# One group ahead instead of two: reordering the software pipeline of a two-layer attention and feed-forward kernel

## Chip, cores, metric

One core of one Trainium2 chip. The metric is the time of one execution on the device, in microseconds (us), as a median of several runs. One execution per kernel was also recorded by the hardware profiler; its span is about 2 us below the time of the same execution. PE is TensorE, DVE VectorE, ACT ScalarE, POOL GpSimd, SP the engine that issues most DMAs.

## The reference, cut

Two layers, each an attention block A and a feed-forward block B with residuals, with the same weights in both layers; sequence 2048, width 1024, 32 heads of 32, hidden width 3584, bf16. Attention looks at eight positions only: itself and 2, 4, ... 14 back.

```python
idx = pos[:, None] - off[None, :]            # off = 0, 2, ..., 14
logits = einsum("bhsd,bhswd->bhsw", q, kg) * scale   # kg, vg: gathered windows of k, v
attn = softmax(where(mask, logits, -1e9))
o = einsum("bhsw,bhswd->bhsd", attn, vg)
x = x + A(layernorm(x)); x = x + B(layernorm(x))     # B: gelu(x @ w1 + b1) @ w2 + b2
x = x + A(layernorm(x)); x = x + B(layernorm(x))
```

## The kernel before

The sequence is cut in four groups of T = 512 positions; a step n is one group in one layer, so there are eight steps. Everything is kept transposed (features on partitions). Nearly all matmuls stream 512 columns. The parts of a step:

- *Layernorm*: sums by matmuls with a matrix of ones, `s1` (centring, DVE), `s2` (squares, ACT, and their sums, PE), `s3` (Ln, Exp on ACT, scaling in two halves on DVE).
- *Projections* `gen_qkv`: 8 chunks of q and k, then 8 of v (24 "units" of 8 matmuls). For each q, k chunk DVE builds the products for all eight window positions, and PE reduces them over a head with a 128x32 stationary matrix, four tiles side by side.
- *Value part* `av_chunk`, 8 chunks: the softmax weights go to DRAM and come back by a broadcast DMA (1 MB a chunk), DVE multiplies them with the windows of vT and adds the eight positions up.
- *Output projection* `gen_wo`, then FFN1 (28 units) and FFN2 (16 units).

```python
xnp = tile_pool(bufs=2); attp = tile_pool(bufs=1)     # kT and vT: one buffer each
wpool = tile_pool(bufs=4); prodp = tile_pool(bufs=2); abcp = tile_pool(bufs=3)
def acc_tile(): return psum.tile([P, T], F32, name="acc", bufs=4)
for g in range(NG):                                   # all x loads first, on the SP queue
    nc.sync.dma_start_transpose(xg[g][:], ...)
...
def av_a(n, c):                                       # cut
    d = ABC_Q.dma_start(abc[...], src)                # broadcast, paced by PE progress (mark)
    nc.vector.tensor_tensor(out=abc[:], in0=abc[:], in1=win(vT[:, c, :]), op=ALU.mult)
def av_b_dve(n, c):                                   # three adds: 8 -> 4 -> 2 -> 1 positions
...
def pipelined():                                      # run(gen, sides): sides[u] is issued after unit u
    ln_a[0].all()
    run(gen_qkv(0, ...), layernorm of step 1)
    run(gen_qkv(1, ...), layernorm of step 2, av_chunk(0, c) at unit 2c)
    for n in range(N):
        if n + 2 < N:
            if n >= 1:
                run(gen_ffn1(n - 1, ...), av_chunk(n + 1, c) at units 1, 6, 11, ...)
                run(gen_ffn2(n - 1), last av_chunks, first layernorm of step n + 2)
            run(gen_wo(n))
            run(gen_qkv(n + 2, ...), second layernorm of step n;   # for n == 0 also
                                     av_chunk(1, c) at unit 2c)
        ...                                           # the two last steps: cut
```

So the value part of step n+1 is done one round before its output projection. Instructions are then placed on their engines by a scheduler that may move ready work forward; each engine runs its list in order.

Of the kernel before, what the change touches and what calls it, by code (L numbers as in the profile page):

```python
# [18 lines left out]
def kernel(  # L19
# [56 lines left out]
    prodp = ctx.enter_context(tc.tile_pool(name="prodp", bufs=2))  # L76
    smp = ctx.enter_context(tc.tile_pool(name="smp", bufs=1))
    abcp = ctx.enter_context(tc.tile_pool(name="abcp", bufs=3))
    hpool = ctx.enter_context(tc.tile_pool(name="hpool", bufs=1))
    iop = ctx.enter_context(tc.tile_pool(name="iop", bufs=1))  # L80
    psum = ctx.enter_context(tc.tile_pool(name="psum", bufs=1, space=PSUM))
    dram = ctx.enter_context(tc.tile_pool(name="dram", bufs=2, space=DRAM))

# [17 lines left out]
    last_pe = [None]  # L101
    mark = [None]
# [5 lines left out]
    PE_AV = False  # L108
    last_seg = [None]
# [19 lines left out]
    for g in range(NG):  # L129
        nc.sync.dma_start_transpose(xg[g][:], x_in[g * T:(g + 1) * T, :].rearrange("s (k p) -> s k p", p=P))  # L130
# [4 lines left out]
    nc.vector.memset(eps_t[:], EPS)  # L135
    smat = const.tile([P, NCH, H], BF16, name="smat")
# [17 lines left out]
    with nc.allow_non_contiguous_dma(reason="tiny bias loads"):  # L154
        nc.sync.dma_start(b1_bf[:], B_b1.rearrange("(j p) -> p j", p=P))
        nc.sync.dma_start(b2_bf[:], B_b2.rearrange("(j p) -> p j", p=P))
    b1T = const.tile([P, KF], F32, name="b1T")
    b2T = const.tile([P, KD], F32, name="b2T")
    nc.vector.tensor_copy(b1T[:], b1_bf[:])
    nc.vector.tensor_copy(b2T[:], b2_bf[:])  # L160
# [13 lines left out]
    def rstd_from(src, prev, preload):  # L174
        rstd = lnp.tile([P, T], F32, name="rstd", bufs=2)
        if preload:
            pl = nc.scalar.preload_act_table_set(LN_SET)
            dep_order(pl, prev, "table preload after squares")
            prev = pl
        ln_i = nc.scalar.activation(rstd[:], src, ACT.Ln, bias=eps_t[:], scale=1.0 / D)  # L180
        dep_order(ln_i, prev, "ln after squares/preload")
        nc.scalar.activation(rstd[:], rstd[:], ACT.Exp, scale=-0.5)  # L182
        return rstd

    class LN:
        def __init__(self, g, preload=False):
            self.g = g
            self.xn = None
            self.preload = preload

        def s1(self):
            x = xg[self.g]
            ps_sum = aux_f32()
            for c in range(KD):
                mm(ps_sum[:], lhsT=ones_bf[:], rhs=x[:, c, :], start=(c == 0), stop=(c == KD - 1))
            self.xn = xnp.tile([P, KD, T], BF16, name="xn")
            nc.vector.scalar_tensor_tensor(  # L197
                out=self.xn[:], in0=ps_sum[:].unsqueeze(1).to_broadcast([P, KD, T]), scalar=-1.0 / D,
                in1=x[:], op0=ALU.mult, op1=ALU.add)

        def s2(self):
            xn = self.xn
            self.ps_sq = aux_f32()
            for c in range(KD):
                sq = lnp.tile([P, T], BF16, name="sq", bufs=2)
                self.last_sq = nc.scalar.activation(sq[:], xn[:, c, :], ACT.Square)  # L206
                mm(self.ps_sq[:], lhsT=ones_bf[:], rhs=sq[:], start=(c == 0), stop=(c == KD - 1))

        def s3(self):
            xn = self.xn  # L210
            rstd = rstd_from(self.ps_sq[:], self.last_sq, self.preload)
            KH2 = KD // 2
            for hh in range(2):
                nc.vector.tensor_tensor(out=xn[:, hh * KH2:(hh + 1) * KH2, :], in0=xn[:, hh * KH2:(hh + 1) * KH2, :],  # L214
                                        in1=rstd[:].unsqueeze(1).to_broadcast([P, KH2, T]), op=ALU.mult)
            self.ps_sq = None
# [26 lines left out]
    def gen_qkv(n, ln, v_first):  # L243
# [56 lines left out]
        pending = None  # L300
        for c4 in range(NCH // 4):
            wq = load_w(wqkv_v, c4 * 4 * P)
            wk = load_w(wqkv_v, D + c4 * 4 * P)
            for cc in range(4):
                c = c4 * 4 + cc
                psq = gemm_chunk(wq, cc, xn, KD)
                qT = qp.tile([P, T], BF16, name="qT")
                nc.scalar.copy(qT[:], psq[:])  # L308
                yield
                psk = gemm_chunk(wk, cc, xn, KD)  # L310
                nc.scalar.copy(kT[:, c, HALO:], psk[:])  # L311
                prod = prodp.tile([P, W, T], BF16, name="prod")
                nc.vector.tensor_tensor(out=prod[:], in0=qT[:].unsqueeze(1).to_broadcast([P, W, T]), in1=win(kT[:, c, :]), op=ALU.mult)  # L313
                if pending is not None:
                    qk_reduce(*pending)
                pending = (c, prod)
                yield
        if g + 1 < NG:
            nc.scalar.copy(khalo[:], kT[:, :, T:T + HALO])
        if v_first:  # L320
            stn["finish"] = (lambda pend=pending: finish(pend))
        else:
            yield from v_part(after_first=(lambda pend=pending: finish(pend)))

    def av_a(n, c):
        stn = st[n]
        vT = stn["vT"]
        a_d = stn["a_d"]
        if c == 0:
            stn["oT"] = attp.tile([P, NCH, T], BF16, name="oT", bufs=2)  # L330
            stn["abc"] = {}
        abc = abcp.tile([P, W, T], BF16, name="abc")
        for hi in range(HPC):
            src = a_d[HPC * c + hi:HPC * c + hi + 1, :, :].rearrange("o w t -> o (w t)").to_broadcast([DH, W * T])
            d = ABC_Q.dma_start(abc[hi * DH:(hi + 1) * DH, :, :].rearrange("p w t -> p (w t)"), src)  # L335
            if mark[0] is not None:
                dep_sync(d, mark[0], "pace abc broadcast with PE progress")
        nc.vector.tensor_tensor(out=abc[:], in0=abc[:], in1=win(vT[:, c, :]), op=ALU.mult)  # L338
        stn["abc"][c] = abc

    def av_b_dve(n, c):
        stn = st[n]
        pv = stn["abc"].pop(c)
        oT = stn["oT"]
        nc.vector.tensor_tensor(out=pv[:, 0:4, :], in0=pv[:, 0:4, :], in1=pv[:, 4:8, :], op=ALU.add)  # L345
        nc.vector.tensor_tensor(out=pv[:, 0:2, :], in0=pv[:, 0:2, :], in1=pv[:, 2:4, :], op=ALU.add)  # L346
        nc.vector.tensor_tensor(out=oT[:, c, :], in0=pv[:, 0, :], in1=pv[:, 1, :], op=ALU.add)

    def av_b_pe(n, c):
        stn = st[n]  # L350
        pv = stn["abc"].pop(c)
        oT = stn["oT"]
        ps = acc_tile()
        for w_ in range(W):
            mm(ps[:], lhsT=ident[:], rhs=pv[:, w_, :], start=(w_ == 0), stop=(w_ == W - 1))
        nc.scalar.copy(oT[:, c, :], ps[:])
# [18 lines left out]
    def gen_ffn1(n, ln):  # L375
        xn = ln.xn
        hT = hpool.tile([P, KF, T], BF16, name="hT")
        st[("h", n)] = hT
        for j4 in range(KF // 4):
            wt = load_w(w1_v, j4 * 4 * P)  # L380
            for jj in range(4):
                j = j4 * 4 + jj
                ps = gemm_chunk(wt, jj, xn, KD)
                nc.scalar.activation(hT[:, j, :], ps[:], ACT.Gelu_apprx_tanh, bias=b1T[:, j:j + 1])  # L384
                yield

    def gen_ffn2(n):
# [3 lines left out]
        for i2 in range(KD // 2):  # L391
            pss = [acc_tile(), acc_tile()]
            for kh in range(2):
# [3 lines left out]
                for ii in range(2):  # L397
                    for k in range(KH):
                        m = mm(pss[ii][:], lhsT=w2t[:, k, ii * P:(ii + 1) * P], rhs=hT[:, kh * KH + k, :],
                               start=(kh == 0 and k == 0), stop=(kh == 1 and k == KH - 1))  # L400
                        if k == 0:
                            mark[0] = m
                    if kh == 1:
                        i = i2 * 2 + ii
                        nc.vector.scalar_tensor_tensor(out=x[:, i, :], in0=pss[ii][:], scalar=b2T[:, i:i + 1], in1=x[:, i, :],  # L405
                                                       op0=ALU.add, op1=ALU.add)
                    yield
# [22 lines left out]
    def seq_all():  # L430
        for n in range(NSTEP):
# [22 lines left out]
    def ln_sides(sides, ln, u0, du):  # L454
        add_side(sides, u0, ln.s1)
        add_side(sides, u0 + du, ln.s2)
        add_side(sides, u0 + 2 * du, ln.s3)

    def pipelined():
        N = NSTEP  # L460
        ln_a = {}
        ln_b = {}
        nc.scalar.preload_act_table_set(LN_SET)
        ln_a[0] = LN(0)
        ln_a[0].all()
# [7 lines left out]
        for c in range(NCH):  # L473
            if PE_AV:
                add_side(sides, 2 * c, (lambda c=c: av_a(0, c)))
                add_side(sides, 2 * c + 5, (lambda c=c: av_b_pe(0, c)))
# [3 lines left out]
        for n in range(N):  # L480
            g = n % NG
            has_qkv = (n + 2 < N)
            if has_qkv:
                if n >= 1:
# [18 lines left out]
                    ln_sides(sides, ln_a[n + 2], 5, 3)  # L503
# [7 lines left out]
                if n == 0:  # L511
                    ln_sides(sides, ln_b[n], 2, 4)
                    for c in range(NCH):
                        if PE_AV:
                            add_side(sides, 2 * c, (lambda c=c: av_a(1, c)))
                            add_side(sides, 2 * c + 5, (lambda c=c: av_b_pe(1, c)))
# [7 lines left out]
            elif n == N - 2:  # L524
# [12 lines left out]
                ln_sides(sides, ln_b[n], 1, 3)  # L537
# [17 lines left out]

    if NG >= 4 and NSTEP >= 4:
        pipelined()
    else:
        seq_all()
# [30 lines left out]
```

## Time and profile before

| | before |
|---|---|
| median of 4 runs | 1437.43 us (1436.34 to 1438.71) |
| PE busy | 1333.3 us, 93% of the span |
| first projection matmul | 30.3 us |
| PE waits of over 20 us | 34.6 us (to 158.6), 26.9 us (to 254.4) |

From the page of the kernel before: first the busy time by engine, then three rows of the span in 40 slices of 36 us, each digit the busy share in tenths (PEclk is the granted clock of TensorE in tenths).

```profile
PE 1333.3 (93%) x6413; PEld 590.5 (41%) x6542; DVE 715.4 (50%) x540; ACT 412.4 (29%) x648; POOL 147.6 (10%) x337
...
PE   4994593999999999999999999999999999999996
...
DVE  3669589436663467336673376444574274201000
...
PEclk7997797899999999999999999999999999999998
```

PE is full from the ninth slice to the last but one. Nearly all its waste lies in the first eight slices and at the end. The waits of PE name it (columns: engine, tile, line waiting, then what released it; us in total, times, longest):

```profile
PE acc L123 <- ACT vT L288: 61.4, 2, 34.6
...
PE acc L123 <- DMA wt<-in_B_w_dram: 2.7, 1, 2.7
```

The two value-eviction waits are two holes in the prologue (the time before the first feed-forward matmuls). The windows view shows who worked meanwhile (busy us and instructions of PE, PEld, DVE, ACT, POOL, then clock, DMA share and GB/s):

```profile
124.00:158.60 34.60, 0.03 (x2) 0.00 (x0) 34.15 (x29) 1.88 (x4) 10.09 (x20) 0.53 0.66 162
226.30:254.40 28.10, 1.27 (x6) 0.49 (x5) 27.49 (x25) 1.84 (x4) 8.15 (x16) 0.60 0.74 173
265.50:1102.00 836.50, 831.95 (x4007) 368.99 (x4087) 448.59 (x337) 254.60 (x402) 94.15 (x190) 1.00 0.77 196
```

In both holes DVE is over 97% busy and PE is all but empty. Most of DVE's work there is the value part of the step before; in the first hole the rest is the softmax of step 1 and the scaling of step 2's layernorm:

```profile
124.48 2.28 DVE L214 TENSOR_TENSOR xn<-xn,rstd 128x2048 bf16<-128x2048 bf16 x1
...
134.67 2.29 DVE L214 TENSOR_TENSOR xn<-xn,rstd 128x2048 bf16<-128x2048 bf16 x1
```

vT has one buffer, so the v chunks of the next step cannot leave their four accumulators until the last product of the step before has read vT; with four accumulators full PE stops. After 265 us the same engines overlap and PE idles half a per cent.

One more reading, the start of an output projection in the steady state, first PE, then DVE (start, duration):

```profile
527.17 13.98 PE L123 MATMUL acc<-oT,wt 128*128 128x512 bf16 x62
...
535.44 0.42 DVE L347 TENSOR_TENSOR oT<-abc 128x512 bf16<-128x512 bf16 x1
```

The last oT of the newer step is begun 8.3 us and done 8.7 us after this output projection began. Harmless here: it uses the oT of the older step.

### The profile page before, as it was taken

What the parts mean: (1) busy time and instruction counts of PE and PEld (TensorE: products, weight loads), DVE (VectorE), ACT (ScalarE), POOL (GpSimd) and SP (SyncE); (2) the same over time, 40 slices, a digit from 0 to 9 for tenths busy, and PEclk for the clock granted to TensorE, in tenths of its full rate; (3) what the DMA queues carried; (4) which work ended last, traced back from release to release, by engine and by line L of the source; (5) the groups of instructions that cost most, each with busy time, mean ns of one, the idle gap of its engine ahead of it and who ended that gap; (6) DMA issues with size and microseconds to landing.
All of it is one profiled execution on the core that took longest, in us unless ns stands there. A gap on an engine that the chain in (4) does not pass through costs nothing.

```text
span 1437.2 us, 15240 instructions
## 1 busy us (share of the span) xinstructions
PE 1333.3 (93%) x6413; PEld 590.5 (41%) x6542; DVE 715.4 (50%) x540; ACT 412.4 (29%) x648; POOL 147.6 (10%) x337
## 2 busy tenths in 40 slices
PE   4994593999999999999999999999999999999996
PEld 1341241444444444444444444444434444444443
DVE  3669589436663467336673376444574274201000
ACT  2332130421243113431144123432134210720411
POOL 1022122120011100121002100121003010000000
PEclk7997797899999999999999999999999999999998
DMA  9377488699359962899449973699638885455551
GB/s 234 118 200 191 121 205 212 165 234 229 128 158 245 232 198 88 223 244 223 138 147 243 236 202 117 184 246 220 196 116 224 230 196 175 143 144 168 169 144 40
DMA packets 277349, 263.17 MB, mean 183 GB/s; under 512 B 28960, under 2 KB 266528, under 8 KB 269088
## 3 DMA queue, kind: packets, MB, share of 16 engines
q1 hardware_dynamic: 263968, 192.96, 48.0%
q0 software_dynamic: 13312, 69.22, 21.9%
q8 instruction: 51, 0.84, 0.3%
q14 instruction: 18, 0.15, 0.0%
HBM read 251.67 MB, written 6.29 MB: 179 GB/s over the span
## 4 chain that ended last, share of the span: by engine, by line
PE 84%; DVE 8%; DMA 4%; issue 2%; ACT 1%; SPq 1%; DVEq 0%; ACTq 0%
PE acc L123 78%; PE aux L123 3%; DMA wt<-in_B_w_dram 3%; DVE abc L338 3%; PE L L123 2%; DVE prod L313 1%; DVE abc L345 1%; SPq L130 1%; DVE xn L197 1%; DVE abc L346 1%; DVE xn L214 1%; DMA out_dram<-xio 0%; PE aux L126 0%; DMA b_bf<-in_B_b_dram 0%; ACT xio L171 0%
## 5 line engine op out<-in xcount | busy, mean ns | idle before, releaser
L123 PEld LDWEIGHTS <-wt 128*128 128x128 bf16 x5632 | 547.5, 98 | 746.5 <-issue 104.0
L123 PE MATMUL acc<-xn,wt 128*128 128x512 bf16 x3247 | 742.1, 382 | 68.8 <-ACT vT L288 61.4
L123 PE MATMUL acc<-hT,wt 128*128 128x512 bf16 x1760 | 393.7, 379 | 1.8
L384 ACT ACTIVATE hT<-acc,b1T 128x512 bf16<-128x512 f32 x224 | 153.1, 687 | 259.1 <-PE acc L123 251.2
L338 DVE TENSOR_TENSOR abc<-abc,vT 128x4096 bf16<-128x4096 bf16 x64 | 146.3, 2287 | 156.6 <-DMA abc<-a_d 156.6
L313 DVE TENSOR_TENSOR prod<-qT,kT 128x4096 bf16<-128x4096 bf16 x64 | 146.0, 2289 | 83.7 <-ACT kT L311 83.7
L405 DVE SCALAR_TENSOR_TENSOR xg<-acc,b2T,xg 128x512 bf16<-128x512 f32 x64 | 48.0, 749 | 278.1 <-PE acc L123 278.0
L335 POOL DMA_DIRECT2D abc<-a_d x256 | 124.4, 495 | 510.6 <-PE acc L123 320.8
L206 ACT ACTIVATE sq<-xn 128x512 bf16<-128x512 bf16 x128 | 73.0, 623 | 181.7 <-DVE xn L197 135.1
L123 PE MATMUL acc<-oT,wt 128*128 128x512 bf16 x500 | 112.5, 379 | 0.6
L214 DVE TENSOR_TENSOR xn<-xn,rstd 128x2048 bf16<-128x2048 bf16 x32 | 73.0, 2285 | 40.6 <-ACT rstd L182 40.6
L197 DVE SCALAR_TENSOR_TENSOR xn<-aux,xg 128x4096 bf16<-128x4096 f32 x16 | 70.8, 4424 | 43.7 <-PE aux L123 35.9
L371 DVE TENSOR_TENSOR xg<-acc,xg 128x512 bf16<-128x512 f32 x64 | 44.1, 690 | 79.4 <-PE acc L123 76.8
L308 ACT CAST qT<-acc 128x512 bf16<-128x512 f32 x64 | 37.5, 586 | 147.0 <-PE acc L123 139.9
L345 DVE TENSOR_TENSOR abc<-abc 128x2048 bf16<-128x2048 bf16 x64 | 78.3, 1223 | 1.8
L276 POOL DMA_DIRECT2D a_d<-a x32 | 18.6, 618 | 502.9 <-DVE a L273 502.9
L123 PE MATMUL aux<-sq,ones_bf 128*128 128x512 bf16 x128 | 47.3, 392 | 12.7 <-ACT sq L206 12.5
L311 ACT CAST kT<-acc 128x512 bf16<-128x512 f32 x64 | 37.4, 584 | 68.4 <-PE acc L123 63.8
L288 ACT CAST vT<-acc 128x512 bf16<-128x512 f32 x64 | 36.8, 586 | 62.9 <-PE acc L123 62.3
L123 PEld LDWEIGHTS <-ones_bf 128*128 128x128 bf16 x256 | 25.6, 100 | 54.7 <-issue 27.7
L171 ACT COPY xio<-aux 128x1024 bf16<-128x1024 bf16 x16 | 16.2, 1011 | 110.1 <-PE aux L126 84.0
L346 DVE TENSOR_TENSOR abc<-abc 128x1024 bf16<-128x1024 bf16 x64 | 44.1, 689 | 1.7
(43 smaller groups left out, 251.4 us busy)
## 6 DMA issues: line engine op xcount, KB each, us to landing
abc<-a_d POOLq DMA_DIRECT2D x256, 256.0 KB, 8.0
wt<-in_B_w_dram SPq DMA_DIRECT2D x56, 1024.0 KB, 5.9
wt<-in_B_w_dram SPq DMA_DIRECT2D x64, 896.0 KB, 10.4
wt<-in_A_wqkv_dram SPq DMA_DIRECT2D x48, 1024.0 KB, 5.1
wt<-in_A_wo_dram SPq DMA_DIRECT2D x16, 1024.0 KB, 5.8
out_dram<-xio SPq DMA_DIRECT2D x16, 256.0 KB, 2.2
a_d<-a POOLq DMA_DIRECT2D x32, 64.0 KB, 2.4
xg<-in_A_x_dram SPq DMA_TRANSPOSE x4, 6.4
```

Source lines behind the costliest of these rows:

```text
L123: return pe_chain(nc.tensor.matmul(out_ap, *args, **kwargs), _seg(out_ap))
L197: nc.vector.scalar_tensor_tensor(out=self.xn[:], in0=ps_sum[:].unsqueeze(1).to_broadcast([P, KD, T]), scalar=-1.0 / D, in1=x[:], op0=ALU.m ...
L206: self.last_sq = nc.scalar.activation(sq[:], xn[:, c, :], ACT.Square)
L214: nc.vector.tensor_tensor(out=xn[:, hh * KH2:(hh + 1) * KH2, :], in0=xn[:, hh * KH2:(hh + 1) * KH2, :], in1=rstd[:].unsqueeze(1).to_broadc ...
L313: nc.vector.tensor_tensor(out=prod[:], in0=qT[:].unsqueeze(1).to_broadcast([P, W, T]), in1=win(kT[:, c, :]), op=ALU.mult)
L335: d = ABC_Q.dma_start(abc[hi * DH:(hi + 1) * DH, :, :].rearrange("p w t -> p (w t)"), src)
L338: nc.vector.tensor_tensor(out=abc[:], in0=abc[:], in1=win(vT[:, c, :]), op=ALU.mult)
L345: nc.vector.tensor_tensor(out=pv[:, 0:4, :], in0=pv[:, 0:4, :], in1=pv[:, 4:8, :], op=ALU.add)
L346: nc.vector.tensor_tensor(out=pv[:, 0:2, :], in0=pv[:, 0:2, :], in1=pv[:, 2:4, :], op=ALU.add)
L371: nc.vector.tensor_tensor(out=x[:, i, :], in0=ps[:], in1=x[:, i, :], op=ALU.add)
L384: nc.scalar.activation(hT[:, j, :], ps[:], ACT.Gelu_apprx_tanh, bias=b1T[:, j:j + 1])
L405: nc.vector.scalar_tensor_tensor(out=x[:, i, :], in0=pss[ii][:], scalar=b2T[:, i:i + 1], in1=x[:, i, :], op0=ALU.add, op1=ALU.add)
```

## The change

The intent: work one step ahead instead of two. The prologue then needs one projection stage whose vector work finds no feed-forward matmuls to hide behind, not two. With it come a shorter start (one x load first, biases later, the first layernorm in two column halves), reductions in batches of two chunks, and pins that keep layernorm matmuls at their place. Cut to what runs (options that are off, and helpers for them, are left out):

```diff
-    prodp = tile_pool(name="prodp", bufs=2)
+    prodp = tile_pool(name="prodp", bufs=3)
+    ONE_AHEAD = True
+    RED_BATCH = 2
+    OT_BUFS = 1 if ONE_AHEAD else 2
-    for g in range(NG):
-        nc.sync.dma_start_transpose(xg[g][:], ...)
+    load_x(0)
-    nc.sync.dma_start(b1_bf[:], ...); nc.sync.dma_start(b2_bf[:], ...)
+    def load_bias():   # on the POOL queue, called later
 ...
                 nc.scalar.copy(kT[:, c, HALO:], psk[:])
+                if len(pending) >= RED_BATCH:
+                    flush(0)                    # reduce both waiting chunks
                 prod = prodp.tile([P, W, T], BF16, name="prod")
 ...
-                if pending is not None:
-                    qk_reduce(*pending)
-                pending = (c, prod)
+                pending.append((c, prod))
 ...
+    def pipelined1():
+        lnA = LN(0, cols=(0, T // 2)); lnB = LN(0, cols=(T // 2, T), xn=lnA.xn)   # s1, s2, s3 in turn
+        run(gen_qkv(0, ...), load_x(1), (2), (3) at units 2, 4, 6; layernorm of step 1)
+        run(gen_qkv(1, ...), av_chunk(0, c) at unit 2c;
+                             gen_wo(0) and the second layernorm of step 0 at unit 19)
+        for n in range(1, N):
+            run(gen_ffn1(n - 1, ...), av_chunk(n, c) at units 1, 6, 11, ...)
+            run(gen_ffn2(n - 1), last av_chunks, first layernorm of step n + 1)
+            run(gen_wo(n))
+            run(gen_qkv(n + 1, ...), second layernorm of step n)
+            # the last step: av_chunks every 3.7 units of FFN1, gen_wo in the middle of FFN2,
+            # that FFN2's residual adds pinned behind the last oT
```

## The prediction

> **What bounds it now.** TensorE: the page has PE busy 1333 of 1437 us, and in the windows from 265 to 1422 us it idles about 1%, at clock 1.00 nearly throughout. Its waste (windows, PE waits): the start, 30.3 us before the first projection matmul; two holes, 124 to 158.6 and 227 to 254.4 us, put down to the value eviction (34.6 and 26.9 us); 2.7 us for a weight DMA at 1123; a 15 us tail. In both holes the vector engine is over 97% busy: vT has one buffer, so the value projection of group n+1 waits for group n's last vT product (2.29 us each, 4.6 with its adds, eight per group).
>
> **What the change does.**
> 1. One group ahead, not two. Hole 1 stays, but group 1's value products now spread over FFN1/FFN2 of group 0, as later groups' did already. Hole 2 goes: -27 us, and -2 of cold clock after it (0.78 granted there). The Trainium skill, "TensorE: Matmul & The Clock Gate", Part 1: idleness throttles the clock, activity releases it; the trace agrees.
> 2. Hole 1 loses group 2's layernorm from its vector queue (4.42 + 2 x 2.29 us): -7.
> 3. New exposure: group 0's output projection and second layernorm stand before FFN1 with only half a value projection behind them. Estimate from trace durations: residual add 0.7, sums 0.5, centring 4.4, squares and sums 5.9, Ln and Exp 1.4, first scaling 2.3 = 15 us, less 7 us of value matmuls: +9.
> 4. Start. One x load comes first; the vector queue no longer waits for biases (until 23.5 us, then it ran group 1's centring ahead of group 0's scaling); group 0's layernorm runs in column halves. First projection at 22 to 24 us: -7, of which 2 come back as group 1's layernorm matmuls now run among projections: -5.
> 5. Reduction in batches of two. Eight reduction matmuls with their switches take 0.65 us of each 4.10 us pair; two rounds of four at 0.216 are 0.43. The Trainium skill, "TensorEngine Tiling (Array Packing)", Key Properties, says a mode change drains the array; the timeline agrees. Half of 64 switches at 0.2 us: -6.
> 6. The steady state does the same matmuls, but a group's output projection now follows directly on its own value products. In before's timeline the last oT is done at 535.4 us, 8 us after the output projection began (527.2), harmless as that used the older group. Matmuls of k = 0 to 6 in four accumulators (28 x 0.216 = 6 us) can hide most: +5 over six groups.
> 7. End: value products every 3.7 FFN1 units, before every 3: -1.
>
> **Sum.** 1437 - 29 - 7 + 9 - 5 - 6 + 5 - 1 = 1403; with some luck in ordering, 1400 us (-2.6%), range 1380 to 1428. Faster by over 2%: 0.68; within 2%: 0.30; slower: 0.02.
>
> **What would show it.** One value-eviction wait of 25 to 30 us in place of two; a new PE idle of 5 to 12 us before the first FFN1, released by the layernorm; first projection at 22 to 24 us; reductions in runs of 16; PE busy sum nearly unchanged; at each output projection a PE wait for oT under 3 us.
>
> **What would make it wrong.** Step 6: if the vector queue puts the last products behind FFN2's residual adds and the matmul order has no filler, each group stalls 5 to 8 us: +30, and the gain is gone. Step 4: if the later x transposes (4.2 us of issue each) hold up weight loads in their queue, 5 to 7 us come back. Step 2: if value products are paced by their broadcast DMA, hole 1 does not shrink.

## The result, and the profile after

The changed kernel takes 1404.44 us (median of 9 runs, 1401.88 to 1411.86), the kernel before 1438.10 us (median of 12). The ratio is 0.9771, with a 95% interval of 0.9754 to 0.9788. Ratios here and below are the mean time of one kernel's fast runs over that of the other's of the same rounds, so not quite the ratio of the medians.

The page after, the same rows:

```profile
PE 1330.6 (95%) x6430; PEld 594.3 (42%) x6558; DVE 719.5 (51%) x544; ACT 408.7 (29%) x654; POOL 149.5 (11%) x339
...
PE   6991799999999999999999999999999999899996
...
DVE  4769543764446733567336663466444674633000
...
PEclk8996899999999999999999999999999999999998
```

The work is the same (PE 1330.6 against 1333.3 us); three near-empty stretches became two. The waits of PE after:

```profile
PE acc L129 <- ACT vT L375: 31.8, 1, 31.8
...
PE acc L129 <- DMA wt<-in_B_w_dram: 6.6, 2, 3.9
PE acc L129 <- DVE xn L293: 6.1, 2, 3.8
```

One value-eviction wait instead of two; a new wait for the scaled layernorm (3.8 us before the first FFN1, 2.3 us at the start); and more waiting for weight DMAs than before. The remaining hole, and the stretch between the first output projection and the first FFN1, by windows:

```profile
112.00:143.90 31.90, 0.07 (x2) 0.03 (x1) 31.18 (x28) 1.91 (x4) 12.51 (x22) 0.56 0.88 200
159.20:174.70 15.50, 11.25 (x48) 4.64 (x48) 7.53 (x4) 9.27 (x16) 0.00 (x0) 0.98 0.43 135
```

The start of an output projection after, PE and DVE:

```profile
440.65 14.27 PE L129 MATMUL acc<-oT,wt 128*128 128x512 bf16 x63
...
445.82 0.43 DVE L448 TENSOR_TENSOR oT<-abc 128x512 bf16<-128x512 bf16 x1
```

The last oT is begun 5.2 us and done 5.6 us after the output projection began, which now needs it, yet the projection takes only 0.3 us more than before (14.27 against 13.98). Each output chunk sums eight matmuls, k = 0 to 7, and only k = 7 needs the last oT. In the instruction order 28 matmuls come first, k = 0 to 6 of four chunks in the four accumulators (one of the records is missing); the first k = 7 starts at 446.69 us, 0.4 us after the last oT is done. So PE doesn't wait for oT at all. The 0.3 us comes later: the fifth chunk's first matmul starts 0.3 us late, at 447.85 us, just as DVE's residual add of the first chunk has ended (447.80) and freed its accumulator.

Marks in both traces show where the time came from:

| mark, us | before | after | difference |
|---|---|---|---|
| first projection matmul | 30.3 | 20.6 | -9.7 |
| hole 1 begins | 124.0 | 112.0 | -12.0 |
| hole 1 ends | 158.6 | 143.9 | -14.7 |
| first GELU of FFN1 | 266.1 | 178.1 | -88.0 |
| first transpose of the last output tiles | 1422.3 | 1390.4 | -31.9 |
| end | 1437.2 | 1405.4 | -31.8 |

From the first GELU to the last tiles 56 us are given back. Most of it is work that has merely moved: the projections and first layernorm of step 2 stood ahead of the first FFN1 before and follow it now. From the trace's 0.216 us a matmul that is 208 x 0.216 = 45 us and 8 reductions of 0.55 us, 49 us in all. The other 7 us are loss. The waits for feed-forward weights in this stretch, with the half clock after them, cost 10.9 us in the changed kernel (6.6 of waiting; then half clock for 3.4 and for 5.2 us, which loses half of each) and 4.4 us in the kernel before (2.7 and 3.4 us at half clock): 6.5 us more. What the batched reductions give back in this stretch goes about even with gaps of under 1 us; I have not separated these.

### The profile page after: what moved, and what is told of

The parts are those of the page before. It is cut to its first block, busy times and chain, and to the rows that moved or that the text cites. A ratio compares the mean times of both kernels' runs of the same rounds, so it can differ in the third digit from the quotient of the medians.

```text
span 1405.4 us, 15288 instructions
## 1 busy us (share of the span) xinstructions
PE 1330.6 (95%) x6430; PEld 594.3 (42%) x6558; DVE 719.5 (51%) x544; ACT 408.7 (29%) x654; POOL 149.5 (11%) x339
## 4 chain that ended last, share of the span: by engine, by line
PE 85%; DMA 6%; DVE 5%; ACT 2%; issue 1%; POOL 0%; DVEq 0%; ACTq 0%; POOLq 0%
PE acc L129 79%; PE aux L129 4%; DMA wt<-in_B_w_dram 3%; PE L L129 2%; DVE abc L439 1%; DMA out_dram<-xio 1%; DMA abc<-a_d 1%; ACT sq L268 1%; DVE xn L256 1%; DVE abc L446 1%; ACT xio L188 1%; DVE xn L293 1%; DVE prod L407 0%; DMA xg<-in_A_x_dram 0%; DMA a_d<-a 0%
## 5 line engine op out<-in xcount | busy, mean ns | idle before, releaser
L129 PE MATMUL acc<-xn,wt 128*128 128x512 bf16 x3249 | 738.7, 381 | 14.5 <-DVE xn L293 6.1
L436 POOL DMA_DIRECT2D abc<-a_d x256 | 124.0, 493 | 491.1 <-PE acc L129 366.0
L129 PE MATMUL acc<-oT,wt 128*128 128x512 bf16 x503 | 114.3, 382 | 32.7 <-ACT vT L375 31.8
L268 ACT ACTIVATE sq<-xn 128x512 bf16<-128x512 bf16 (+1 forms) x136 | 74.1, 597 | 223.8 <-DVE xn L256 200.5
L293 DVE TENSOR_TENSOR xn<-xn,rstd 128x2048 bf16<-128x2048 bf16 (+1 forms) x34 | 73.1, 2160 | 34.9 <-ACT rstd L199 34.9
L256 DVE SCALAR_TENSOR_TENSOR xn<-aux,xg 128x4096 bf16<-128x4096 f32 (+1 forms) x17 | 70.9, 4173 | 37.3 <-PE aux L129 37.3
L129 PE MATMUL aux<-sq,ones_bf 128*128 128x512 bf16 (+1 forms) x136 | 48.2, 373 | 3.5 <-ACT sq L268 2.6
```

The source lines that it names most:

```text
L129: return pe_chain(nc.tensor.matmul(out_ap, *args, **kwargs), _seg(out_ap))
L256: nc.vector.scalar_tensor_tensor(out=self.xn[:, :, c0:c1], in0=self.tot[:, c0:c1].unsqueeze(1).to_broadcast([P, KD, n]), scalar=-1.0 / D, ...
L268: self.last_sq = nc.scalar.activation(sq[:, c0:c1], xn[:, c, c0:c1], ACT.Square)
L293: nc.vector.tensor_tensor(out=xn[:, hh * KH2:(hh + 1) * KH2, c0:c1], in0=xn[:, hh * KH2:(hh + 1) * KH2, c0:c1], in1=rstd[:, c0:c1].unsquee ...
L436: d = ABC_Q.dma_start(abc[hi * DH:(hi + 1) * DH, :, :].rearrange("p w t -> p (w t)"), src)
```

## The experiments

Each is an edit of the changed kernel. e1 to e4 share a chip and its runs of the kernel before (median 1439.97 us); e5 to e8 share another set (1437.00), e9 to e11 another (1438.53), and e12 has its own (1440.23). So compare within a set, or by ratio. The changed kernel itself has the ratio 0.9771 (0.9754 to 0.9788) in its first set and 0.9750 in e4's.

### e4: the changed kernel again

> The changed kernel unaltered, for the same chip and rounds as its variants: 1404 us, give or take 4. The profile should show either no, one or two weight-DMA waits of 2 to 4 us of PE in the first FFN2 unit of some group: if these come from chance overlap of the broadcast and the weight load, they sit in other groups than 556 and 1216 us; if they come from the program, in the same ones.

Measured: 1403.49 us (1402.97 to 1403.97), ratio 0.975 (0.9736 to 0.9765). Its profile spans 1402.2 us and has weight waits at 1209.6 us (0.8) and 1219.9 us (3.2), and none at 556 us, where the first profile had 2.7 us. So the late one, in the last step, is in both; the other came by chance. Each costs more than it lasts: the 20 us stretch from 540 us held 73 matmuls in the first profile where its neighbours hold 92, so 19 x 0.216 = 4.1 us for a wait of 2.7. The granted clock says why; the wait ended at 556.1 us:

```profile
556.30:559.60 3.30, 3.30 (x9) 1.22 (x8) 0.00 (x0) 0.00 (x0) 0.00 (x0) 0.50 1.08 192
```

Nine matmuls in 3.3 us, at half clock.

### e1: two steps ahead again

```diff
-    ONE_AHEAD = True
+    ONE_AHEAD = False
```

> The changed kernel with only the order of the groups put back to two ahead (ONE_AHEAD False, so two oT buffers; a dead constant of 256 bytes is left out to make room). Main theory: the gain is mostly the hole removed from the prologue, so both value-eviction waits of about 27 and 35 us are back and the time is 1424 to 1432 us. Rival: the gain is mostly the earlier start and the batched reductions; then the time stays at or below 1412 us.

Measured: 1441.55 us, ratio 1.001 (0.9993 to 1.0027), 38 us above e4. Waits of PE in it:

```profile
PE acc L129 <- ACT vT L373: 62.3, 2, 33.7
PE acc L129 <- DMA wt<-in_B_w_dram: 8.6, 2, 6.3
PE acc L129 <- DMA wt<-in_A_wqkv_dram: 8.2, 1, 8.2
```

Both holes are back, so the order of the steps is what removed one. The 38 us are not all due to that. The start of e1 is not that of the changed kernel, because this branch issues all x loads at once: PE idles 8.2 us before the first projection, which waits for its weights and begins at 27.2 us, 6.5 us later than in the changed kernel, although the layernorm is in halves. The time is also 10 us above what I expected: the other parts of the change bring nothing in this setting. And 8.6 us of weight waits in FFN1 and FFN2, with a cold clock after each, are of the size of what the batched reductions save; that the one used up the other is argued, not shown. The parts do not simply add. (A dead constant of 256 bytes was left out here and in e7 and e11, to make room.)

### e2: the old start

```diff
+        for g in range(1, NG): load_x(g)
+        load_bias()                          # on the SP queue again
-        lnA = LN(0, cols=(0, T // 2)) ...    # two halves
+        ln_a[0] = LN(0); ln_a[0].all()
-        add_side(sides, 2, (lambda: load_x(1))) ...
```

> The changed kernel with only its start put back: all four x loads and the biases first on the sync queue, the first layernorm in one piece. Theory: the first projection matmul moves from 20.6 us back to 28 to 30 us and the whole time grows by about as much, 7 to 10 us over the changed kernel (1411 to 1415 us), as everything after it is one chain. Rival: the vector engine's backlog in the first hole absorbs the delay, as the hole starts later but ends at the same time: under 3 us.

Measured: 1413.04 us, 9.6 us above e4 (ratio 0.9818). As expected in size. The timelines of PE and DVE show a cause that I had not named:

```profile
27.08 1.89 PE L129 MATMUL acc<-xn,wt 128*128 128x512 bf16 x4 [5.94 <-DMA wt<-in_A_wqkv_dram]
...
23.30 0.18 DVE L176 CAST b1T<-b_bf 128x28 f32<-128x28 bf16 x1 [7.88 <-DMA b_bf<-in_B_b_dram]
24.11 0.17 DVE L177 CAST b2T<-b_bf 128x8 f32<-128x8 bf16 x1 [0.64 <-DMA b_bf<-in_B_b_dram]
24.19 4.49 DVE L293 TENSOR_TENSOR xn<-xn,rstd 128x2048 bf16<-128x2048 bf16 x2
```

The first weights stand behind four x transposes and two bias loads in the SP queue; they are issued at 21.0 us and land 6.0 us later. The biases stand behind the same transposes and hold DVE, so the first half of the scaled layernorm is done only at about 26.5 us, 0.5 us before the weights. In e1 the biases have another queue and the layernorm is in halves, and it is ready at 22.3 us; still the projection begins at 27.2 us, with the weights. So in both runs, with four x loads ahead of the weights, the start is at 27 us, though the layernorm is 4 us sooner in one; with the weights behind one x load it is 20.6 us, and then the layernorm ends last (a wait of 2.3 us, above). What the halves and the late biases are worth in that order was not run alone. The rest of the 9.6 us comes soon after: where the hole ends, e2 is 8.7 us behind the changed kernel (152.6 against 143.9 us).

### e3: reductions one by one

```diff
-    RED_BATCH = 2
+    RED_BATCH = 1
```

> The changed kernel with reductions one chunk at a time (RED_BATCH 1). The prediction put the batching at 6 us. In the trace of the changed kernel only 17 runs of 16 reduction matmuls are found beside 30 runs of 8 (before: 58 of 8 and 12 of 4), so 23 switches fewer at 0.2 us: theory 3 to 5 us slower than the changed kernel, about 1408 us. Rival: switches cost nothing that lies on the chain, within 1 us of the changed kernel.

Measured: 1409.15 us, 5.7 us above e4 (ratio 0.9793, interval 0.9774 to 0.9812, against 0.9750, 0.9736 to 0.9765). By the spans of the two profiles it is 3.9 us. The batch in the changed kernel and single reductions in e3, on PE:

```profile
82.89 1.05 PE L129 MATMUL L<-prod,smat 128*32 128x512 bf16 x16
83.87 7.08 PE L129 MATMUL acc<-xn,wt 128*128 128x512 bf16 x31
```

```profile
83.94 0.62 PE L129 MATMUL L<-prod,smat 128*32 128x512 bf16 x8
84.49 3.63 PE L129 MATMUL acc<-xn,wt 128*128 128x512 bf16 x16
```

From start to start 16 reduction matmuls take 0.98 us, eight take 0.55 us, so two single runs take 0.12 us more. The matmuls ahead of a run lose another 0.1 us each time: 16 of them take 3.56 us from start to start (84.49 to 88.05 in e3), where 16 x 0.2157 are 3.45. (A count of x31 for 32 is a record missing from the trace.) Only 17 runs of 16 stand in the changed kernel, beside 30 of 8, as the scheduler puts other matmuls between the two chunks of a batch.

### e5: the output projection in program order

```diff
                     m = mm(ps[:], lhsT=wt[:, k, ...], rhs=oT[:, k, :], ...)
+                    if prev_m is not None:
+                        dep_order(m, prev_m, "output projection in program order")
+                    prev_m = m
```

> The changed kernel with one thing added: the matmuls of the output projection are chained in program order, so the k = 7 matmul of its first chunk may not be passed by matmuls of the next chunks. In the changed kernel the last oT of a group lands 5.2 us after its output projection began and PE waits only 0.3 us, because 21 matmuls of k = 0 to 6 of three chunks come first. Theory: without this filler PE waits about 5.2 - 1.5 = 3.7 us in each of groups 2 to 7, so 15 to 25 us over the changed kernel (1418 to 1428 us), with waits of PE for the vector engine's oT. Rival: the scheduler moves the vector engine's last products forward when it sees the wait, or the slack was there anyway: within 5 us of the changed kernel.

Measured: 1431.17 us, ratio 0.9955, 27 us above the changed kernel. (The expectation's 21 matmuls of three chunks is a miscount: the trace has 28 of four, as above.) The wait is there in the second to the seventh step, 4.0 us in three of them, near the 3.7 computed, 1.7 to 1.8 us in the others (two of these have the transposes of output tiles as filler):

```profile
PE acc L129 <- DVE oT L448: 17.2, 6, 4.0
```

But 17 us of waiting cost 27 us. The step of the reading above, now:

```profile
443.57 1.67 PE L129 MATMUL acc<-oT,wt 128*128 128x512 bf16 x7
449.23 15.35 PE L129 MATMUL acc<-oT,wt 128*128 128x512 bf16 x57 [3.98 <-DVE oT L448]
```

57 matmuls at 0.216 us are 12.3 us, but they take 15.35: after 4 us of idling the clock is at half for the next 5.9 us, which loses 2.9 us (the 14 matmuls here come 0.42 us apart):

```profile
449.23:455.10 5.87, 5.87 (x14) 2.08 (x14) 1.38 (x2) 0.00 (x0) 0.00 (x0) 0.50 0.00 0
```

The Trainium skill, "TensorE: Matmul & The Clock Gate", Part 1, says that an idle window of about 3.4 us throttles the clock and about as much activity releases it. The clock halves and comes back, but less idling was enough: the waits of 2.7 us in the changed kernel (e4, above) and in the kernel before (granted clock 0.50 from 1126.2 to 1129.6 us, just after it) were followed by about 3.4 us at half clock. So the filler that the scheduler found is worth most of the change's gain, and the worst case that the prediction named (+30 us) was real.

### e6: the adds of step 0 on TensorE

The hole of 31.8 us looked like a backlog of DVE, and PE idles in it. So the adds of step 0 went to PE, as eight matmuls with the identity.

```diff
-            add_side(sides, 2 * c, (lambda c=c: av_chunk(0, c)))
+            add_side(sides, 2 * c, (lambda c=c: av_a(0, c)))
+            add_side(sides, 2 * c + 5, (lambda c=c: av_b_pe(0, c)))
```

> The changed kernel with the window adds of group 0 moved from the vector engine (2.35 us a chunk) to eight identity matmuls a chunk on TensorE (8 x 0.216 = 1.73 us), which idles in the hole. Theory: the hole of 31.8 us is the vector engine's backlog; the products of group 0 then end up to 8 x 2.35 = 19 us sooner and the time falls by 10 to 18 us (1386 to 1394 us). Rival: the broadcast DMA (1 MB a chunk, near 5 us each in this stretch) paces the products just as much; then the vector engine waits for DMA instead and the time falls by less than 6 us.

Measured: 1432.04 us, ratio 0.9967, 28 us worse. Neither theory foresaw it. The hole is gone, but each pair of q and k chunks now has two waits of PE:

```profile
111.66 0.61 PE L129 MATMUL L<-prod,smat 128*32 128x512 bf16 x8 [3.00 <-DVE prod L407]
113.87 3.59 PE L129 MATMUL acc<-abc,ident 128*128 128x512 bf16 x8 [1.59 <-DVE abc L439]
117.26 4.75 PE L129 MATMUL acc<-xn,wt 128*128 128x512 bf16 x16
```

Projection, product, reduction, value product and identity matmuls became one serial chain over PE, ACT and DVE, of 13 us a pair for 4 us before, at a cold clock (eight identity matmuls in 3.4 us from start to start). Work moved to an idle engine stands in that engine's order, and whatever it waits for, all behind it waits too. About the hole this run says nothing.

### e9: step 0 without its adds (wrong result)

```diff
-        nc.vector.tensor_tensor(out=pv[:, 0:4, :], ...)      # 1.22 us
-        nc.vector.tensor_tensor(out=pv[:, 0:2, :], ...)      # 0.69 us
+        if n > 0:                                            # both, but not for step 0
```

> Wrong on purpose: the changed kernel without the first two window adds of group 0 (1.22 and 0.69 us a chunk on the vector engine, 15.3 us in all); everything else as it was. The run before this one, with the adds on TensorE, put a new serial chain into the projection and so did not tell whether the hole is the vector engine's backlog. Theory: it is, so the hole of 31.8 us shrinks by 10 to 15 us and the time falls by as much (1389 to 1394 us). Rival: the broadcast DMA paces the products, the vector engine then waits for it, and the hole shrinks by less than 5 us.

Measured: 1402.93 us, ratio 0.9737; the hole is 29.5 us. My theory falls: 15 us taken from the busiest engine shortened the hole by 2.3 us, and the ratio (0.9711 to 0.9763) is within the noise of the changed kernel's. The waits of DVE in it from 110 to 145 us:

```profile
DVE abc L439 <- DMA abc<-a_d: 8.1, 3, 5.4
```

DVE now waits for the broadcast. In the changed kernel it never does in this hole. The DMA engines' busy share from 100 us to the end of the hole is 0.88 in the changed kernel and 0.98 in e9 (the number before the last; changed kernel first):

```profile
100.00:143.90 43.90, 11.97 (x70) 4.87 (x66) 41.44 (x35) 3.65 (x8) 14.44 (x26) 0.68 0.88 207
...
100.00:142.00 42.00, 13.08 (x82) 5.17 (x81) 29.40 (x22) 3.64 (x8) 12.81 (x23) 0.72 0.98 232
```

### e12: and with half the broadcast (wrong result)

```diff
+            nw = W // 2 if n == 0 else W        # load windows 0 to 3 only in step 0
-        nc.vector.tensor_tensor(out=abc[:], in0=abc[:], in1=win(vT[:, c, :]), op=ALU.mult)
+        # step 0: two half products, both from the loaded half, so DVE's work stays
```

> Wrong on purpose: the run without the adds of group 0, and with only half of each broadcast of group 0 loaded (0.5 MB a chunk for 1 MB); the product keeps its length, as two halves that both read the loaded half, so the vector engine's work is that of the run without the adds. That run left a hole of 29.5 us with the vector engine waiting for the broadcast. Theory: the broadcast DMA was then the limit, so the hole now shrinks to 12 to 20 us and the time to 1385 to 1394 us. Rival: the hole is set by the order of instructions and not by either load; then hole and time stay within 3 us of the run without the adds (29.5 us, 1403 us).

Measured: 1387.27 us, ratio 0.9634. The wait of PE:

```profile
PE acc L129 <- ACT vT L375: 14.8, 1, 14.8
```

The hole halves, and within it DVE is again busy without a gap (25.74 of 26 us from 100 us on). So in the changed kernel the hole has two limits of nearly the same length: DVE's chunks of 4.65 us (from product to product), which hold it open for 31.8 us, and the broadcast, which holds it open for 29.5 us once DVE is relieved (e9). In the changed kernel only the first of them shows. Relieving DVE alone gives almost nothing. Half the broadcast with all the adds was not run; as DVE never waits for the broadcast in the changed kernel's hole, I would expect nothing from it.

### e10: the adds on TensorE with slack

```diff
+        pools["abcx"] = ...                                 # three more broadcast buffers, prologue only
+            add_side(sides, min(2 * c + 12, 19), (lambda c=c: av_b_pe(0, c)))
-        ps = acc_tile()
+        ps = aux_f32()
```

> The adds of group 0 on TensorE again, now with slack: three more broadcast buffers during the prologue, the identity matmuls of chunk c seven projection units later (at unit 2c+12, at most 19), and the sums in the two spare accumulators. If the first attempt failed only for its tight order, the hole now shrinks and the time falls by 6 to 14 us against the changed kernel (1390 to 1398 us). Rival: TensorE still waits in order for products that come late, as the broadcast DMA is near its limit here; then the time is not below 1402 us.

Measured: 1412.99 us (1407.79 to 1417.16), ratio 0.9819; the rival's number was right, its reason only in part. The hole of 31.8 us is gone. In its place PE waits 14.5 us for a projection weight load and 5.2 us later on, and runs 64 identity matmuls (64 x 0.216 = 14 us), so nothing is won. With six buffers the broadcasts run ahead, and the weight load shares the DMA engines with them:

```profile
119.94 3.50 PE L129 MATMUL acc<-xn,wt 128*128 128x512 bf16 x8 [14.54 <-DMA wt<-in_A_wqkv_dram]
```

The Trainium skill, "DMA: Bandwidth & Descriptors", Issuing engines are not separate DMA queues, says that DMAs of all issuing engines run on the same 16 DMA engines and interleave. This trace agrees: the broadcasts are issued by POOL and the weights by SP, the DMA engines' share is 1.03 meanwhile, and this load takes 33.9 us from issue to landing, where the same load took 13.1 us in the changed kernel.

### e7: five weight buffers

```diff
-    wpool = tile_pool(name="wpool", bufs=4)
+    wpool = tile_pool(name="wpool", bufs=5)
```

> The changed kernel with five weight buffers for four (a dead constant of 256 bytes left out to make room). The PE waits for a weight DMA of FFN1 and FFN2 near 1210 to 1220 us, in every run of the changed kernel, and now and then in another group. Theory: a load issued one tile earlier (6.9 us) lands in time, these waits go, -3 to -6 us against the changed kernel. Rival: the DMA engines are at their limit over the whole of FFN1 with the broadcasts (share above 1.0), so a deeper prefetch only moves the wait: within 2 us.

Measured: 1397.70 us, ratio 0.9723 (0.9705 to 0.9741). The wait that was 6.6 and 4.0 us in the two profiles of the changed kernel:

```profile
PE acc L129 <- DMA wt<-in_B_w_dram: 0.8, 1, 0.8
```

So the weight waits were a matter of prefetch depth. By medians the gain is 5.8 us against e4, by ratios 3.9 (against e4, whose interval this one just touches) to 6.9 us; that the waits shrink to 0.8 us is plain in the trace. The DMA engines have room for the deeper prefetch over FFN1 and FFN2.

### e8 and e11: four output tiles, and both together

```diff
-    iop = tile_pool(name="iop", bufs=1)
+    iop = tile_pool(name="iop", bufs=4)
```

> The changed kernel with four output tiles for one. The last 15 us are four rounds of copy (1.0 us) and store (2.1 us), each waiting for the one before. Theory: with four tiles the copies run back to back and the stores overlap, -5 to -7 us, the same tail as in the kernel before, so no part of what the change did. Rival: stores of one queue do not overlap: -3 us or less.

Measured: 1398.25 us (1395.45 to 1404.37), ratio 0.973 (0.9707 to 0.9753). From the first of the last transposes to the end it takes 8.2 us instead of 15. The tail was the same in the kernel before, so this is no part of what the change did.

In e11 the five weight buffers leave no room for more output tiles, so the last four tiles use the broadcast buffers, idle by then.

```diff
+        if final:
+            xo = abcp.tile([P, W, T], BF16, name="abc")[...][:, 0:D]
```

> The changed kernel with five weight buffers and with the four last output tiles in the broadcast buffers, free by then, so that the last stores overlap. The two gains measured alone (about 5 us each) should add, as they lie in different stages: 1391 to 1395 us. Rival: less than the larger of the two, 1397 us or more.

Measured: 1393.49 us (1392.49 to 1397.61), ratio 0.9679 (0.9655 to 0.9703), correct. It beats both kernels; the two gains add.

## Why the prediction was right, point by point

The prediction said 1400 us and its sum 1403; measured were 1404.4 and 1403.5. The mechanism was right. The terms:

1. *Hole 2 goes, -29.* Right. One value-eviction wait is left, and e1, with the order put back, has both again. It is 38 us slower, of which 6.5 us are its later start and some its weight waits.
2. *Hole 1 loses a layernorm, -7.* The size was off: the hole went from 34.6 to 31.8 us, -2.8. The hole ends 5.0 us sooner than the earlier start alone explains (-14.7 against -9.7), but the 16 layernorm matmuls that left (3.5 us of PE) had stood before the hole, so it also begins sooner. (e3, without the batches, ends the hole 0.5 us later than e4, so at most that much of the 5.0 is due to them.) e9 and e12 show besides that the broadcast DMA is right behind DVE there, as the prediction's last paragraph had feared.
3. *New exposure, +9.* The chain from the output projection's end to the first FFN1 is 15.4 us (159.2 to 174.6), as estimated (15). The net is smaller: 48 matmuls, 10.4 us, ran in it, not only the 32 v matmuls, as the 16 of the layernorm itself were needed anyway. That leaves 15.4 - 10.4 = 5 us, of which 3.8 is the wait shown (5 to 12 were forecast); after it the clock is at half for another 2.8 us (0.51 from 174.6 to 177.4 us), about 1.4 us more.
4. *Start, -5 net.* The first projection came at 20.6 us, not 22 to 24, so -9.7 gross; e2 puts the whole effect at 9.6 us with nothing absorbed later. The cause was only half named: I saw the bias wait and the order on DVE, which did set the 30.3 us of the kernel before, but e1 and e2 show that behind these the weights after the x transposes hold the start at 27 us.
5. *Batches, -6.* Right in size (e3: 5.7 us by the timed medians, 3.9 by the profiles), although only 17 of the intended 32 runs of 16 formed.
6. *Output projection behind its own products, +5.* The filler is the one named, 28 matmuls in four accumulators, but it hides all of the wait and not most: what is left is 0.3 us in each of three steps, about 1 us in all, and that for a free accumulator. e5 shows the cost without it, 27 us.
7. *End, -1.* Wrong in sign and small: the last step's weight wait is 3.9 us (3.2 and 0.8 in e4), against 2.7.

Not in the prediction at all: weight waits by chance in other steps, with cold clock afterwards, which e7 removes. They, term 7 and the missing part of term 2 took what terms 3, 4 and 6 had been too pessimistic about, so the sum came out closer than its parts; that closeness is luck. What stays open is how to shorten the remaining hole in a correct kernel: e6 and e10 both failed, and e9 with e12 show that less vector work gives little unless the broadcast bytes fall too. A second vT buffer, which would remove the wait itself, was not run. The trace lets one doubt it: what PE does first after the hole is the output projection of step 0, whose last input oT is done only at 145.5 us, and the 32 value matmuls that could move into the hole (7 us) now fill the wait for the second layernorm.

## What to carry to other kernels

A pipeline that runs further ahead than its buffers allow pays in the prologue: count how many stages must run before the first one that hides the slow engine's work, and take the smallest depth that keeps the steady state full. When the depth shrinks, look at every consumer that now follows directly on its producer, and see whether the in-order list of the consumer has independent work before the first wait; a 4 us wait cost 7 us here (e5). Before relieving the engine that is 97% busy, look at what is second: here the DMA engines would hold the hole open for 29.5 us (e9) where the vector engine held it for 31.8, and relieving the first alone gave almost nothing.

## What the Trainium skill lacked or had wrong

- "TensorE: Matmul & The Clock Gate", Part 1, says that the clock is throttled after an idle window of about 3.4 us. Here two waits of 2.7 us were each followed by about 3.4 us at half clock (the changed kernel at 553 us, the kernel before at 1123 us), and so was one of 2.3 us (e1, granted clock 0.50 from 325.8 to 329.1 us), while after one of 2.5 us the clock stayed full (e2, 1.00 from 1228.6 to 1237.5 us); so it is not the length of the single wait alone. What a longer wait costs here: 57 matmuls after 4 us took 15.35 us instead of 12.3 (e5).
- "TensorEngine Tiling (Array Packing)", Key Properties, says that a mode change drains the array, without a cost. Here one excursion to the 128x32 tile and back costs about 0.2 us beyond its matmuls: 0.12 us by the runs themselves (16 reduction matmuls 0.98 us from start to start, eight 0.55 us) and 0.1 us in the matmuls ahead (e3).
- "Perfetto Trace Analysis", Identifying the Most-Contended Engine, advises to optimize the engine with the highest occupancy first. It lacks the case of a second load right behind: taking 15 us off the 98% busy vector engine moved the hole from 31.8 to 29.5 us, as the DMA share rose from 0.88 to 0.98 (e9).
- "DMA: Bandwidth & Descriptors" says that DMAs of all issuers interleave, but no page gives the size of a wait that a deeper prefetch of one stream causes in another: a 1 MB weight load took 33.9 us from issue to landing beside broadcasts into six buffers (e10), 13.1 us beside those into three (changed kernel), where the median for such loads was 5.1 us; PE waited 14.5 us for it.
